# Loading half of an output projection in four-row pieces, and reordering the heads' outputs to match, in a two-layer decode kernel

## The chip, the cores and the metric

The kernel runs on one core of a Trainium2 chip. The metric is the device time of one execution in microseconds (us), from three timed runs. A core has a matrix engine (TensorE, "PE" in the profile, with its weight loads listed apart as "PEld"), a vector engine (VectorE, "DVE"), a scalar engine (ScalarE, "ACT"), a general engine (GpSimd, "POOL") and a sync engine ("SP"), whose queue issues nearly all of this kernel's loads. Each engine has its own list of instructions, and semaphores make one engine wait for another. The kernel lets PE write its products to PSUM tiles, from which DVE or ACT read them.

## The reference

Two identical decoder layers are applied to four sequences of one token each. The cache and the weights are the same in both layers. Cut to what matters:

```
B, D, Hq, Hkv, Sk, Dh, F = 4, 512, 32, 8, 4096, 128, 1792      # bfloat16

def A(x):                                   # attention over a cache
    q = (x @ wq)                            # 32 query heads of 128
    k, v = repeat(k_cache, 4), repeat(v_cache, 4)   # 8 key heads, 4 query heads each
    p = softmax(q @ k.T * Dh ** -0.5)       # 4096 positions
    o = p @ v                               # (B, Hq, 1, Dh)
    return o.reshape(B, 1, Hq * Dh) @ wo    # wo: 4096 x 512

def M(x):
    return (gelu(x @ w_gate) * (x @ w_up)) @ w_down

x = x + A(layernorm(x)); x = x + M(layernorm(x))
x = x + A(layernorm(x)); x = x + M(layernorm(x))
```

[...] The projection `wo` is 4 MB and stays on the chip once it is loaded.

## The kernel before

**Order of the work.** The kernel handles sequence after sequence. `attend_first` does layer 1 of sequence 0. `attend` is called three times; each call does layer 2 of sequence b-1 beside layer 1 of sequence b, so that the K and V tiles of a sequence are read close together. `attend_last` does layer 2 of the last sequence and ends in the output projection of layer 2 for all four sequences. `dense_first`, `dense` and `dense_last` are the feed-forward parts. The order is written out by hand (the kernel turns automatic scheduling off).

**Loads.** SP issues the loads in program order. K and V come in tiles of 512 KB, each partition reading 16 adjacent rows of 256 bytes, which is 4 KB in one piece. A V slot is handed to the next tile when its last matmul is done (`ring.pump`, L708); K tiles are issued from L518. `load_rest` (L158) loads all the weights that are needed after the first attention: first `wo` in four loads of 1 MB (L161), then the gate, up and down weights. For `wo` the row index is split as (head i, partition p), so each partition gets one row of 512 numbers, 1 KB, per query head.

**Attention values.** Class `Values` walks through V tiles (`step`). For most key heads the probabilities are the stationary operand and V is streamed past them (`stream_v`, L791); afterwards DVE transposes the result (`turn_v`, L799), sums it (L806) and scales it (L807) into the output array, in which every query head is one column of 128 partitions: `OT_bf` for layer 1, `OT2_bf` for layer 2 (four columns a head, one for each sequence). For the other heads V is the stationary operand (L859), and one DVE instruction (L680) scales. `step(n, hold=True)` puts off the DVE part until `flush()`.

**Output projection.** Six of the eight key heads go through `RowProj`: the head's column is stationary and a row block of `wo` is streamed (L405); four heads run in four 32-column strips of PE. `split` (L412 on ACT, then L413 on DVE) turns the four strips into a pair of terms, and `onto` adds them to the result of `OutProj`, which handles the last two key heads with `wo` as the stationary operand (L275). At the end `add_x` (L425) adds the projection to the residual.

**In `attend_last`** the two key heads of each pair are done in the order (2,3), (0,1), (4,5), 6, 7. The steps around the change are: `vals.step(8, hold=True)`, `soft_turn(p1)`, `vals.flush()`, the second group's swap of probabilities, two ACT fills and an ACT table load (L1291), `vals.step(4)` for heads 4 and 5, `rows.heads` for pairs (2,3) and (0,1), `vals.step(2)` for head 6, `rows.heads` for (4,5), `rows.split()`, then head 7 in two steps with head 6's projection between them, `rows.onto(proj)`, and head 7's projection.

Of the kernel before, what the change touches and what calls it, by code (L numbers as in the profile page):

```python
# [8 lines left out]
FP32 = mybir.dt.float32  # L9
# [6 lines left out]
P = 128  # L16

LN_EPS = 1e-5
QD = 4
QS = P // QD  # L20
WIDE = 32
WEIGHT = 64
# [3 lines left out]
GH = 4  # L26
# [10 lines left out]
def kernel(  # L37
# [24 lines left out]
    NT = C // CH  # L62
# [6 lines left out]
    TG = GH * NT  # L69
# [15 lines left out]
    ps_sm = ctx.enter_context(tc.tile_pool(name="ps_sm", bufs=1, space=bass.MemoryType.PSUM))  # L85
# [3 lines left out]
    dq = nc.sync  # L89

    wq_sb = [wts.tile([P, KD, HG * Dh], BF16, name=f"wq_sb{g}") for g in range(NG)]
    wo_sb = wts.tile([P, Hq, D], BF16, name="wo_sb")
# [9 lines left out]
    wo_dram = A_wo.rearrange("(i p) n -> p i n", p=P)  # L102
# [7 lines left out]
    ident_bf = const.tile([P, P], BF16, name="ident_bf")  # L110
# [38 lines left out]
    def cache_tile(cache, b, kvh, t):  # L149
        if whole(b, kvh):  # L150
            return cache[b, kvh].rearrange("(p t c) d -> t p c d", t=NT, p=P)[t]
        return cache[b, kvh].rearrange("(t p c) d -> t p c d", t=NT, p=P)[t]

    def load_wq(g):
        n = HG * Dh
        dq.dma_start(out=wq_sb[g][:], in_=wq_dram[:, :, g * n:(g + 1) * n])

    def load_rest():  # L158
        n = Hq // 4
        for i in range(4):  # L160
            dq.dma_start(out=wo_sb[:, i * n:(i + 1) * n], in_=wo_dram[:, i * n:(i + 1) * n])  # L161
        dq.dma_start(out=wg_sb[:], in_=B_w_gate.rearrange("(k p) n -> p k n", p=P))
        dq.dma_start(out=wu_sb[:], in_=B_w_up.rearrange("(k p) n -> p k n", p=P))
        wd_dram = B_w_down.rearrange("(k p e) n -> p k e n", p=P, e=2)
        wd_pairs = wd_sb.rearrange("p (k e) n -> p k e n", e=2)
        for lo, hi in zip(WD_PARTS, WD_PARTS[1:]):
            if hi - lo > 1:
                own = slice(lo // 2, hi // 2)
                dq.dma_start(out=wd_pairs[:, own], in_=wd_dram[:, own])
            else:  # L170
                dq.dma_start(out=wd_sb[:, lo], in_=wd_dram[:, lo // 2, lo % 2])
# [307 lines left out]
    def busy(count, unread, by=None, start=True, lhsT=None):  # L479
        rhs = wg_sb[:, 0] if by is None else by  # L480
        for _ in range(count):
            nc.tensor.matmul(unread, lhsT=ident_bf[:] if lhsT is None else lhsT, rhs=rhs[:, :unread.shape[1]], start=start,  # L482
                             stop=start, skip_group_check=True)
# [98 lines left out]
    def scores(sc, g, t, runs=together):  # L582
        for run in runs:
            scores_of(sc, g, [(s, t) for s in run])
# [224 lines left out]

    class Values:  # L810
        def __init__(self, layer, b, tiles, prob, dst, keeps=(), streamed=(), paired=(), sums=None, park=(),
                     last_bank=None, off_ot=False, last_width=WEIGHT):
            self.streamed, self.sums, self.park = streamed, sums or {}, park
            self.paired, self.last_bank, self.off_ot = paired, last_bank, off_ot
            self.last_width = last_width
            self.layer, self.b, self.tiles, self.n = layer, b, list(tiles), 0
            self.prob, self.dst, self.keeps = prob, dst, keeps
            self.seen, self.ot, self.late = {}, None, []
# [65 lines left out]
        def unit(self, kvh):  # L884
            pair = [2 * (kvh // 2), 2 * (kvh // 2) + 1]
            alone = kvh in self.streamed and kvh not in self.paired
            return [kvh] if self.tiles[-1][0] in pair or alone else pair

        def scale(self, ot, unit, rden):
            n, s = len(unit), unit[0] % GH  # L890
            if unit[0] in self.streamed:
                turn_v(ot, n)
                return sum_v(ot, self.dst(unit[0], n), rden[:, s:s + n], n)
            scaled(self.dst(unit[0], n), ot[:, s % 2:s % 2 + n, :rep], rden[:, s:s + n])
# [5 lines left out]
    class Streamed:  # L900
# [30 lines left out]
        def sum(self):  # L931
            kvh, ps = self.sums.pop(0)
            g, s = divmod(kvh, GH)
            sum_v(ps, self.dst(kvh, 2), self.prob[g][1][:, s:s + 2], 2)
# [22 lines left out]
    hp = 2 * rep  # L957

    def attend_first():

        b, (gx, gy) = 0, first_groups[0]
        prob1 = {}
        keys = Keys(b, (gx, gy))
        kept, own, other, _ = two(b)
        last = one(b)[-1][0]
        vals = Values(1, b, one(b), prob1, dst1(b), keeps=kept,
                      streamed=[h for h in range(Hkv) if h != last],
                      paired=[h for h in range(Hkv) if h // 2 != last // 2])
        ring.extend(1, b, one(b))
        load_wq(gx)  # L970
        keys.load_heads(GH)
        load_wq(gy)
        keys.load(TG)
        ring.pump()
        make_identity(nc, ident_bf[:])
        build_consts()
        xT_ps = ps_sm.tile([P, KD, B], BF16, name="xT_ps", tag="sm")
        for k in range(KD):
            nc.tensor.transpose(xT_ps[:, k, :], x_bf[:B, k * P:(k + 1) * P], ident_bf[:B, :B])
        nc.vector.tensor_copy(out=xb[:, :, :B], in_=xT_ps[:])  # L980
# [12 lines left out]
        q_first(gx)  # L993
        q_build(q1_bf[:, gx, :, b])
        sc1 = new_scores()
        for s in range(GH):
            keys.turn(NT)
            for t in range(NT):
                scores_of(sc1, gx, [(s, t)])
        p0 = soft(sc1)  # L1000
        q_first(gy)
        soft_turn(p0)
        q_build(q1_bf[:, gy, :, b])
        pe, den = soft_swap(p0), soft_den(p0)
        keys.turn()
        prob1[gx] = (pe, soft_recip(den))
        keys.turn(3)
        vals.step(2)
        sc1 = new_scores()
        scores(sc1, gy, 0, last_alone)  # L1010
        keys.turn(4)
        vals.step(3)
        scores(sc1, gy, 1, last_alone)
        vals.step(3, hold=True)
        p0 = soft(sc1)
        vals.flush()
        soft_turn(p0)
        prob1[gy] = (soft_swap(p0), soft_recip(soft_den(p0)))
        vals.step(TG)
        assert vals.left() == 0  # L1020
        load_rest()
        scr = Scratch()
        early = Early(b + 1, second_groups[b])
        heads, twice = pairs(one(b)), o1(b)
        summed = RowProj(lambda i: twice(i).broadcast_to([P, 2]))
        for h in heads[:-1]:
            summed.heads(h, hp)
        summed.split(scr.words.bitcast(BF16))
        proj = OutProj(o1(b), 1)
        proj.heads(heads[-1], rep)  # L1030
        summed.onto(proj)
        proj.n = Hq - rep
        proj.heads(heads[-1] + rep, rep)
        ring.extend(2, b, own)
        return proj.y, early, scr
# [99 lines left out]
    def attend(b, qy, before, norm, early=None):  # L1135
# [11 lines left out]
        vals1 = Values(1, b, one(b), prob1, dst1(b), keeps=kept1,  # L1147
                       streamed=[gy * GH + s for s in range(GH - 1)], park=apart1,
                       sums={4: (ps_sc, "sc"), 5: (ps_sm, "sm"), 6: (ps_sc, "sc")},
                       last_bank=lambda: ps_sm.tile([P, 2, WEIGHT], FP32, name="ot", tag="sm"))  # L1150

        sc2 = [new_scores(early=True)]
        if early:
# [59 lines left out]
        turn(4)  # L1213
        vals1.step(3)
        scores(sc1, gy, 1, last_alone)
        p0 = soft(sc1)
        vals1.step(3)
        x = swap_tile()
# [4 lines left out]
        heads = pairs(one(b))  # L1223
# [10 lines left out]
        vals1.step(1)  # L1234
        proj = OutProj(o1(b), 1)
        spare = proj.bank[:, KD * WEIGHT:]
        rows.heads(heads[2], rep)
        busy(3, spare)
        vals1.step(1)
        rows.heads(heads[2] + rep, rep)  # L1240
        rows.split()
        busy(5, spare)
        vals1.step(1)
        proj.heads(heads[3], rep)
        vals1.step(1)
# [6 lines left out]
    def attend_last(q_bf, norm, before, late):  # L1252
# [5 lines left out]
        vals = Values(2, b, tiles, prob2, dst2(b),  # L1258
                      streamed=[h for h in range(Hkv) if h != tiles[-1][0]],
                      paired=[h for h in range(Hkv) if h // 2 != tiles[-1][0] // 2],  # L1260
                      last_width=WIDE)
        sc2 = [new_scores(early=True)]
        scores(sc2[0], gx, 0)
        ring.pump_tile(late[0], k_tile(gx * GH + 2, 0))
# [24 lines left out]
        for part in full:  # L1289
            nothing(part[:])  # L1290
        nc.scalar.preload_act_table_set("gelu_apprx_tanh_and_others")  # L1291
        vals.step(4)
        rows.heads(heads[0], hp)
        rows.heads(heads[1], hp)
        vals.step(2)
        rows.heads(heads[2], hp)
        rows.split()
# [1 line left out]
        proj = OutProj(o2, B, WIDE)  # L1299
        proj.heads(heads[3], rep)  # L1300
        vals.step()
        rows.onto(proj)
        proj.n = Hq - rep
        proj.heads(heads[3] + rep, rep)
        part = banks.tile([P, UP_ROWS * WIDE], "ur")
        nothing(part[:])
        spare = ps_sc.tile([P, 512], FP32, name="spare", tag="sc")
# [265 lines left out]
```

## Time and profile before

| | |
|---|---|
| three timed runs | 267.55, 268.86, 269.77 us (median 268.86) |
| the profiled execution: device time | 268.99 us |
| its span, first to last instruction | 267.2 us |
| PE / DVE / ACT busy | 195.1 / 182.2 / 66.0 us |
| DMA packets, bytes | 30732, 103.05 MB, mean 386 GB/s |
| packets of the main load queue as a share of 16 engines' span | 95.7% |
| packets under 2 KB | 7144 |
| chain that ended last, by engine | DMA 51%, PE 21%, DVE 16%, SP's queue 6% |
| `wo` loads, issue to landing | 12.0 us median |
| V tiles, issue to landing | 8.5 us median |

The profile shows one execution. A window row gives, for a stretch in us from the span's start, the busy time of each engine (number of instructions in brackets), the granted PE clock, the busy share of the DMA engines and GB/s. A timeline row gives start, duration of the group, engine, source line, operation, output and inputs, shapes and count; in square brackets stands the idle time before it and what ended it. The chain that ended last is followed back from the last instruction, each step to what released it.

### The profile page before, as it was taken

The page shows a single profiled execution, that of the slowest core. Times are in us where ns is not written, and L with a number is a line of the kernel's source. Part 1 is how long each engine was busy: PE and PEld are TensorE (multiplying, and loading weights), DVE is VectorE, ACT ScalarE, POOL GpSimd, SP SyncE. Part 2 cuts the span into 40 slices and gives each one's busy share as a digit, 9 for nine tenths or more (in the row PEclk, how much of TensorE's full clock was granted, in tenths as well). Part 3 has the DMA queues.
Part 4 walks back from the last instruction along what each step waited for, and adds up shares of the span by engine and source line. Part 5 has one row for each costly group of instructions (what it writes and reads, how often), then busy time and mean ns, then how long its engine had stood idle before and what let it go on. Part 6 is the DMA issues. An engine that isn't in the chain of part 4 may idle for free.

```text
span 267.2 us, 8596 instructions
## 1 busy us (share of the span) xinstructions
PE 195.1 (73%) x3767; PEld 114.8 (43%) x3775; DVE 182.2 (68%) x448; ACT 66.0 (25%) x136; POOL 3.9 (1%) x10
## 2 busy tenths in 40 slices
PE   1396246544689796989678968787788687888884
PEld 1333123322255453557436245464363354553563
DVE  3385955451335899884776998746769996568773
ACT  1001001100222422032323520304136103044642
POOL 2000000000001000000000000000000000000001
PEclk9998555655597959799999985899999979999999
DMA  7999999999994999999999999999999999999940
GB/s 244 432 416 421 423 429 417 408 385 406 413 412 177 394 416 417 420 417 400 390 414 416 416 419 421 416 415 375 403 418 418 421 415 418 420 405 405 413 160 3
DMA packets 30732, 103.05 MB, mean 386 GB/s; under 512 B 2788, under 2 KB 7144, under 8 KB 29672
## 3 DMA queue, kind: packets, MB, share of 16 engines
q1 hardware_dynamic: 30672, 102.51, 95.7%
q8 instruction: 29, 0.48, 0.6%
q14 instruction: 7, 0.06, 0.1%
q10 hardware_dynamic: 24, 0.01, 0.0%
HBM read 102.50 MB, written 0.00 MB: 384 GB/s over the span
## 4 chain that ended last, share of the span: by engine, by line
DMA 51%; PE 21%; DVE 16%; SPq 6%; ACT 3%; issue 3%; DVEq 0%
DMA v_t<-in_A_v_cache_dram 25%; DMA kp<-in_A_k_cache_dram 8%; DMA kw<-in_A_k_cache_dram 8%; PE sc L592 6%; DMA wu_sb<-in_B_w_up_dram 5%; DMA kw<-in_A_v_cache_dram 4%; SPq L161 4%; DVE kp L537 3%; PE ot L859 3%; DVE kw L537 3%; PE y L275 3%; PE so L791 2%; PE q L309 1%; DVE q L315 1%; DVE qb L360 1%
## 5 line engine op out<-in xcount | busy, mean ns | idle before, releaser
L592 PE MATMUL sc<-kw,qb 128*32 128x512 bf16 x244 | 39.6, 446 | 5.2 <-DVE kw L537 2.2
L592 PE MATMUL sc<-kp,qb 128*32 128x512 bf16 x268 | 40.1, 450 | 1.0 <-DVE kp L537 0.2
L592 PEld LDWEIGHTS <-qb 128*32 128x32 bf16 x512 | 23.1, 104 | 39.6 <-issue 21.4
L537 DVE STREAM_TRANSPOSE kw<-kw 128x1024 f32<-128x1024 f32 x32 | 38.0, 1215 | 0.7 <-DMA kw<-in_A_k_cache_dram 0.6
L537 DVE STREAM_TRANSPOSE kp<-kp 128x1024 f32<-128x1024 f32 x32 | 36.7, 1199 | 0.0
L859 PE MATMUL ot<-pe,v_t 128*128 128x32 bf16 (+1 forms) x896 | 30.0, 184 | 5.6 <-DMA v_t<-in_A_v_cache_dram 2.8
L859 PEld LDWEIGHTS <-v_t 128*128 128x128 bf16 x896 | 27.7, 100 | 13.7 <-issue 7.4
L614 ACT ACTIVATE pe<-sc,nl 128x512 bf16<-128x512 f32 x8 | 5.5, 687 | 85.9 <-DVE pe L611 67.6
L791 PE MATMUL so<-v_t,pe 128*32 128x256 bf16 x304 | 15.0, 319 | 13.6 <-DMA v_t<-in_A_v_cache_dram 11.6
L799 DVE STREAM_TRANSPOSE so<-so 128x512 f32<-128x512 f32 (+1 forms) x23 | 13.8, 599 | 11.1 <-PE so L791 11.1
L791 PEld LDWEIGHTS <-pe 128*32 128x32 bf16 x320 | 9.1, 105 | 19.4 <-issue 12.5
L602 DVE TENSOR_REDUCE pe<-sc 128x1 f32<-128x512 f32 x12 | 8.3, 691 | 9.2 <-PE sc L592 9.1
L405 PE MATMUL yr<-wo_sb,OT_bf 128*2 128x512 bf16 (+1 forms) x120 | 10.7, 425 | 4.9 <-DMA wo_sb<-in_A_wo_dram 4.9
L647 PE MATMUL x<-pe,ident_bf 128*32 128x128 bf16 x192 | 5.4, 233 | 11.8 <-DVE pe L622 11.8
L647 PEld LDWEIGHTS <-ident_bf 128*32 128x32 bf16 x256 | 5.3, 100 | 16.1 <-issue 14.1
L791 PE MATMUL so<-v_t,pl 128*32 128x256 bf16 x192 | 9.4, 275 | 3.3 <-DMA v_t<-in_A_v_cache_dram 3.3
L650 ACT CAST pe<-x 128x512 bf16<-128x512 f32 x12 | 7.0, 586 | 17.4 <-PE x L647 17.4
L275 PE MATMUL q<-xb,wq_sb 128*128 128x5 bf16 (+1 forms) x192 | 5.7, 173 | 6.5 <-DMA wq_sb<-in_A_wq_dram 6.5
L353 PE MATMUL qe<-q_bf,ident_bf 128*32 128x16 bf16 (+1 forms) x272 | 5.7, 176 | 5.6 <-DVE q_bf L335 2.9
L622 DVE STREAM_TRANSPOSE pe<-pe 128x512 bf16<-128x512 bf16 x12 | 8.4, 696 | 1.1 <-ACT pe L614 1.1
L275 PEld LDWEIGHTS <-wo_sb 128*128 128x128 bf16 x160 | 7.6, 101 | 3.3 <-DMA wo_sb<-in_A_wo_dram 2.6
L482 PEld LDWEIGHTS <-ident_bf 128*128 128x128 bf16 x63 | 5.2, 99 | 8.7 <-issue 4.3
(172 smaller groups left out, 255.2 us busy)
## 6 DMA issues: line engine op xcount, KB each, us to landing
v_t<-in_A_v_cache_dram SPq DMA_DIRECT2D x89, 512.0 KB, 8.5
kp<-in_A_k_cache_dram SPq DMA_DIRECT2D x32, 512.0 KB, 9.9
kw<-in_A_k_cache_dram SPq DMA_DIRECT2D x24, 512.0 KB, 9.6
wq_sb<-in_A_wq_dram SPq DMA_DIRECT2D x2, 2048.0 KB, 7.7
kw<-in_A_k_cache_dram SPq DMA_DIRECT2D x4, 1024.0 KB, 11.6
v_t<-in_A_v_cache_dram SPq DMA_DIRECT2D x4, 1024.0 KB, 14.2
wo_sb<-in_A_wo_dram SPq DMA_DIRECT2D x4, 1024.0 KB, 12.0
wq_sb<-in_A_v_cache_dram SPq DMA_DIRECT2D x3, 1024.0 KB, 11.8
```

The source lines that it names most:

```text
L161: dq.dma_start(out=wo_sb[:, i * n:(i + 1) * n], in_=wo_dram[:, i * n:(i + 1) * n])
L275: nc.tensor.matmul(dst, lhsT=lhsT, rhs=rhs, start=first, stop=last, skip_group_check=True)
L405: nc.tensor.matmul(self.rows[j:j + x.shape[1]], lhsT=x, rhs=wo_sb[:, i], start=self.n < QD, stop=True, skip_group_check=True)
L537: nc.vector.transpose(out=words, in_=words)
L592: nc.tensor.matmul(sc[s * QS:(s + 1) * QS], lhsT=qb[:, w0:w0 + 2 * W], rhs=kt[:, :, be // 2, :, be % 2], start=(t == 0 and be == 0), stop= ...
L602: nc.vector.tensor_reduce(out=m, in_=sc.rearrange("p c j -> p (c j)"), axis=AX.X, op=ALU.min if norm else ALU.max)
L622: nc.vector.transpose(out=flat, in_=flat)
L647: nc.tensor.matmul(x[a * QS:(a + 1) * QS, s], lhsT=ident_bf[:, s * QS:(s + 1) * QS], rhs=pT[:, a], start=True, stop=True, skip_group_check ...
L650: nc.scalar.copy(out=pe, in_=x.rearrange("p s t c h -> p (s t c h)"))
L791: nc.tensor.matmul(ps[d, :NW * QS], lhsT=x[:, w:w + NW].rearrange("p c h -> p (c h)"), rhs=v[:, i:i + NW, d], start=first and i == 0, stop ...
L799: nc.vector.transpose(out=flat, in_=flat)
L859: nc.tensor.matmul(self.ot[:, s % 2], lhsT=v[:, i, :], rhs=wide(pe[:, s, t * CH + i, :], self.ot.shape[-1]), start=(done == 0 and i == 0), ...
```

## The change: four adjacent rows a partition for key heads 0, 1, 4 and 5

For these four key heads (16 of the 32 query heads, half of `wo`) the load gives partition p the four adjacent rows 4p to 4p+3 of the key head's 512 rows, 4 KB in one piece. The other half is loaded as before. The output columns of these heads must then hold, in partition p, the numbers 4p to 4p+3 of the key head's 512 outputs. `regroup` does this with 16 small matmuls: every fourth column of the identity picks one of four places, for each of four query heads, into one strip of 32 PSUM partitions. One ACT copy writes the result back over the same columns. Where the head's columns are written is unchanged; `regroup` is called twice in each of the five attention passes that end in a projection. Around the calls some steps are reordered.

```diff
+    def by_quads(kvh):
+        return kvh % GH < 2
...
     def load_rest():
         n = Hq // 4
-        for i in range(4):
-            dq.dma_start(out=wo_sb[:, i * n:(i + 1) * n], in_=wo_dram[:, i * n:(i + 1) * n])
+        wo_quads = A_wo.rearrange("(i p j) n -> p i j n", p=P, j=QD)
+        to_quads = wo_sb.rearrange("p (i j) n -> p i j n", j=QD)
+        for kvh in range(0, Hkv, 2):
+            if by_quads(kvh):
+                dq.dma_start(out=to_quads[:, kvh:kvh + 2], in_=wo_quads[:, kvh:kvh + 2])
+            else:
+                i = kvh * rep
+                dq.dma_start(out=wo_sb[:, i:i + n], in_=wo_dram[:, i:i + n])
...
+        def regroup(self):
+            kvh, n = self.due[0][1][0], sum(len(unit) for _, unit in self.due)
+            ps = self.due[-1][0]
+            self.due = []
+            if len(ps.shape) == 3:
+                ps = ps.rearrange("p a b -> p (a b)")
+            o = self.quads[:, kvh * rep:(kvh + n) * rep].rearrange("p (v h) b -> p v h b", h=rep)
+            nb = o.shape[3]
+            turned = ps[:, :n * QD * nb].rearrange("p (v j b) -> p v j b", j=QD, b=nb)
+            for j in range(QD):
+                for h in range(rep):
+                    nc.tensor.matmul(turned[h * QS:(h + 1) * QS, :, j], lhsT=ident_bf[:, j::QD],
+                                     rhs=o[:, :, h], start=True, stop=True, skip_group_check=True)
+            nc.scalar.copy(out=o, in_=turned)
+
         def scale(self, ot, unit, rden):
             n, s = len(unit), unit[0] % GH
+            if self.quads is not None and by_quads(unit[0]):
+                self.due.append((ot, unit))
...
@@ attend_first
         vals.step(3, hold=True)
+        vals.regroup()
         p0 = soft(sc1)
...
-        vals.step(TG)
-        assert vals.left() == 0
+        vals.step(2 * NT + 1)
+        vals.regroup()
+        vals.step(vals.left())
         load_rest()
...
@@ attend
         scores(sc1, gy, 1, last_alone)
+        vals1.regroup()
         p0 = soft(sc1)
...
         spare = proj.bank[:, KD * WEIGHT:]
-        rows.heads(heads[2], rep)
+        vals1.regroup()
+        busy(5, spare)
+        vals1.step(1)
+        rows.heads(heads[2], hp)
+        rows.split()
         busy(3, spare)
-        vals1.step(1)
-        rows.heads(heads[2] + rep, rep)
-        rows.split()
-        busy(5, spare)
         vals1.step(1)
         proj.heads(heads[3], rep)
...
@@ attend_last
         nc.scalar.preload_act_table_set("gelu_apprx_tanh_and_others")
+        vals.regroup()
         vals.step(4)
         rows.heads(heads[0], hp)
         rows.heads(heads[1], hp)
+        vals.regroup()
         vals.step(2)
         rows.heads(heads[2], hp)
         rows.split()
...
         vals.step()
+        proj.n = Hq - rep
+        proj.heads(heads[3] + rep, rep // 2)
         rows.onto(proj)
-        proj.n = Hq - rep
-        proj.heads(heads[3] + rep, rep)
+        proj.heads(heads[3] + rep + rep // 2, rep // 2)
```

`busy(n, ...)` issues n matmuls whose result is not read.

More of the change, by code (lines that the diff above doesn't have):

```diff
@@ L811, in __init__ @@
         def __init__(self, layer, b, tiles, prob, dst, keeps=(), streamed=(), paired=(), sums=None, park=(),
-                     last_bank=None, off_ot=False, last_width=WEIGHT):
+                     last_bank=None, off_ot=False, last_width=WEIGHT, quads=None):
+            self.quads, self.due = quads, []
             self.streamed, self.sums, self.park = streamed, sums or {}, park
@@ L967, in attend_first @@
                       streamed=[h for h in range(Hkv) if h != last],
-                      paired=[h for h in range(Hkv) if h // 2 != last // 2])
+                      paired=[h for h in range(Hkv) if h // 2 != last // 2],
+                      quads=OT_bf.unsqueeze(2))
         ring.extend(1, b, one(b))
@@ L1149, in attend @@
                        sums={4: (ps_sc, "sc"), 5: (ps_sm, "sm"), 6: (ps_sc, "sc")},
-                       last_bank=lambda: ps_sm.tile([P, 2, WEIGHT], FP32, name="ot", tag="sm"))
+                       last_bank=lambda: ps_sm.tile([P, 2, WEIGHT], FP32, name="ot", tag="sm"),
+                       quads=OT_bf.unsqueeze(2))
         sc2 = [new_scores(early=True)]
@@ L1260, in attend_last @@
                       paired=[h for h in range(Hkv) if h // 2 != tiles[-1][0] // 2],
-                      last_width=WIDE)
+                      last_width=WIDE, quads=OT2_bf)
         sc2 = [new_scores(early=True)]
```

## The prediction

> **What bounds the kernel now.** I read the windows first, then the chain that ended last, then the timeline of the two stretches that the chain singles out. The windows (columns: stretch, busy time of PE, PEld, DVE, ACT and POOL, granted PE clock, DMA share, GB/s):
>
> ```profile
> 48.00:50.00 2.00, 1.63 (x34) 1.08 (x34) 0.26 (x1) 1.02 (x2) 0.00 (x0) 0.75 1.03 416
> 56.00:58.00 2.00, 0.94 (x8) 0.23 (x9) 2.00 (x5) 0.00 (x0) 0.00 (x0) 0.50 1.09 386
> 58.00:60.00 2.00, 0.32 (x8) 0.10 (x7) 1.02 (x4) 0.00 (x0) 0.00 (x0) 0.50 1.09 386
> 176.00:180.00 4.00, 3.86 (x79) 3.11 (x78) 1.74 (x5) 0.59 (x1) 0.00 (x0) 1.00 1.03 418
> ```
>
> The DMA engines are full nearly all the time. V tiles move at 416 to 418 GB/s, in pieces of 4 KB; while `wo` moves in pieces of 1 KB (53 to 62 us) the share is as high, 1.09, but the rate is 386. So these pieces cost DMA time, not waiting time. Does that time reach the end? The chain says so:
>
> ```profile
> 59.84 14.06 DMA wu_sb<-in_B_w_up_dram
> 73.94 0.96 PE u L1323 x16
> ...
> 125.34 5.46 DMA v_t<-in_A_v_cache_dram
> ...
> 133.25 0.32 PE qe L353 x16
> ...
> 246.32 11.96 DMA kw<-in_A_v_cache_dram
> ```
>
> The up weights, which queue behind `wo`, land at 73.9 and the feed-forward part of sequence 0 hangs on them; later K and V loads carry the chain until the last half tile of V lands at 258.3. After that a tail of 9 us has no load in it. Whoever lengthens the tail pays in full. Its beginning, in the timeline:
>
> ```profile
> 253.83 1.06 PE L791 MATMUL so<-wq_sb,pl 128*32 128x256 bf16 x32 [0.36 <-ACT pl L650]
> ...
> 254.68 0.18 DVE L807 TENSOR_TENSOR OT_bf<-ov,rden 128x8 bf16<-128x8 f32 x1
> ...
> 254.94 0.73 DVE L799 STREAM_TRANSPOSE so<-so 128x512 f32<-128x512 f32 x1
> ...
> 255.84 0.62 PE L791 MATMUL so<-wq_sb,pl 128*32 128x256 bf16 x16
> 255.97 0.18 DVE L807 TENSOR_TENSOR OT_bf<-ov,rden 128x8 bf16<-128x8 f32 x1
> ...
> 258.73 0.17 DVE L680 TENSOR_TENSOR OT_bf<-ot,rden 128x4 bf16<-128x4 f32 x1 [0.42 <-PE ot L859]
> ...
> 259.54 0.18 DVE L425 TENSOR_TENSOR xb<-XX,y 128x16 bf16<-128x16 f32 x1 [0.63 <-PE y L275]
> ```
>
> PE streams V for heads 4 and 5 at 253.83 while DVE is still summing heads 0 and 1, whose output is complete only at 254.86 (L807). Today nothing on PE needs it before the second half of the row projections.
>
> **The load.** 2.10 MB of `wo` change from 1 KB to 4 KB pieces. At 386 GB/s they take 5.43 us, at the 418 of the V windows 5.02: a gain of 0.4 us. Bounds: nothing, if the piece were not what costs; 0.55 us at the 430 GB/s of the fastest window (34 to 36 us). I take 0.4, from the nearest row (same 4 KB by 128 partitions, same queue). The up weights then land 0.4 us earlier, the K loads of the next sequence are released 0.4 us earlier, and from there the loads run on without a pause to 258.3, so the last landing moves to 257.9.
>
> [...]
>
> **The small matmuls.** Ten regroups add 160 matmuls, 160 weight loads and 10 ACT copies. The trace has no such group, but `q_sums` (L353) has the same form: 128x32 stationary picked out of the identity, a few moving columns, four strips side by side; 16 of them fill 0.32 us of the chain at full clock. Singly such a row lasts 169 ns, so the upper bound is 2.7 us a regroup. I take 0.3, twice that at the 0.5 clock of the first 70 us. For the copy the nearest ACT rows are 0.16 us (128x4) and 0.27 us (128x128); I take 0.2.
>
> **Where they are hidden.** Sequence 0: PE waits for V tiles at 50.6, 51.8 and 53.2 and then for `wo` itself, so both regroups lie beside DMA work. In `attend`, the first regroup stands before the softmax, where PE next idles 0.78 us for DVE (before L647 at 116.94) and ACT has been idle 8.9 us; its inputs were scaled a microsecond earlier. Queued behind it are three V tiles and five dummy matmuls, which end later by 0.3 us and have that gap to use. The second regroup needs head gy1's sum, ready at 120.46, when PE gets there at 120.0: 0.45 us of waiting and 0.3 of work. The five dummies cover the ACT copy, and the displaced row matmuls are the same eight. The projection so ends about 0.6 us later. Behind it on PE are the V tiles whose release lets SP issue loads. The chain shows the price: a tile issued at 125.34 lands 5.46 us later, while a K tile issued into an idle queue (at 83.1) took 3.2. About 2.2 us of queue stand in front of it, so 0.6 us later is no idle DMA, and PE waits for V landings further on in any case. In the last call, V landings already hold PE back at 228.8 and 230.1. I count nothing for all this.
>
> **The tail.** Here nothing hides it. On the time axis of before:
> - Regroup 1 stands ahead of `vals.step(4)`. PE, in order, waits for 254.86, works 0.3, and starts heads 4 and 5 at 255.2 instead of 253.83: 1.4 us late. The ACT copy waits for the table load (254.45 to 255.73), which is early enough for the row projection.
> - Heads 4 and 5 are in PSUM at 256.3 (1.06 us for the 32), and their three DVE steps take 1.2 us (254.94 to 256.15 before): ready at 257.5. PE reaches regroup 2 at 256.95 (0.88 for the V matmuls, 0.86 for 16 row matmuls), waits, and is through at 257.85. Head 6 starts there instead of at 255.84: 2.0 us late.
> - From here PE no longer waits for landings, which gives some of it back. Head 6's output comes 1.57 us after its start (255.84 to 257.41), at 259.4; its 16 projection matmuls take 0.42; head 7's second tile ends near 260.3 and L680 starts near 260.5, against 258.73.
> - Before, `onto`'s four matmuls ran while L680 did; now they stand behind it, between two halves of head 7: 20 matmuls instead of 16, 0.1 us. `split` (ACT 0.59, DVE 0.75) ends near 260.3, just in time.
> - `add_x` (L425) starts at 261.4 against 259.54: 1.9 us late. All that follows is unchanged.
>
> **Sum.** The work that leads up to the tail comes 0.4 us earlier, the tail gets 1.9 us longer: +1.5 us. The profiled execution's 268.99 (span 267.2) becomes 270.5; it stood 0.13 above the median of 268.86, so I predict **270.3 us**, 0.55% more.
>
> **Rivals.**
> - *The tail absorbs it.* If only regroup 1's wait counts and the rest fits into the waits for landings (PE idle before 255.84, 257.04, 258.32), the tail grows by 0.8 instead of 1.9: 269.3; if nothing shows, the load's gain stays: 268.4. For: PE is idle about 1 us in all there. Against: regroup 1 alone moves PE's remaining work past the last landing. Chance 0.18 together.
> - *The load does not get faster*, because the pieces stay at 1 KB or because their size is not what cost: 270.7. The 386 of two windows with a full share speaks against it. Chance 0.08. [...]
> - *The small matmuls do not overlap*, the case that is clearly slower. Place: the two regroups of the tail, where every nanosecond counts, and then the second regroup of each `attend` call, where the loads run dry once PE is more than 2.2 us late. At half overlap (1.3 us each) the tail gains 2 us more: 272.3. At the upper bound of 2.7 us the tail gains 4.8 and each of three calls 0.95 (2.7 and 0.45 of waiting, less 2.2): 278. It decides from 0.9 us a regroup on, where the sum passes 1%. Against it stand the 0.32 us for 16. Chance 0.10.
>
> The forecast itself has 0.64. Two runs of this kernel cannot be told apart within about 1% (the three runs lie 0.8% apart). Below 266.2 lies no case, since the load can give 0.55 us at most: 0.03. Above 271.5 lie the last rival and a part of the forecast's upper side: 0.13. The rest, 0.84, is within 1%. The range reaches from 268.4 (gain kept, tail hidden) to 271.9 (each tail regroup at 0.6 us, the half-clock cost, and the spread of the runs); only the last rival is outside.
>
> **What would show it.** Main-queue packets fall by 1536, and the stretch from 53 to 62 has parts at 416. The up weights land near 73.5 and the last V half near 257.9. In the tail PE idles 0.7 to 1.1 us before regroup 1 and about 0.6 before regroup 2, released by DVE L807's counterpart, and `add_x` starts about 261.0. In `attend` the DMA share stays near 1 after each projection. I am wrong if regroup 1 finds its input ready, if 16 small matmuls take clearly more than 0.3 us, or if the up weights land no earlier.

## The result: 0.58% slower, and the tail hangs on another chain

| | before | after |
|---|---|---|
| device time, median of 14 runs (us) | 269.01 (267.55 to 271.08) | 270.52 (269.57 to 275.02) |
| ratio, 95% interval | | 1.0058 (1.0037 to 1.0080) |
| profiled execution: device time / span (us) | 268.99 / 267.2 | 270.36 / 268.6 |
| packets of the main load queue | 30672 | 29136 |
| packets under 2 KB | 7144 | 5096 |
| first matmul on the up weights (us) | 73.94 | 73.56 |
| last half tile of V landed (us) | 258.28 | 258.42 |
| last `add_x` starts (us) | 259.54 | 260.90 |

One run of 275.02 us lies far from the other 13 and is left out of the ratio. Forecast were 270.3 us and a last `add_x` at about 261.0.

The time is gained early and lost late. The early part stands in the windows of the changed kernel (columns as in the prediction: stretch, busy time of PE, PEld, DVE, ACT, POOL, granted PE clock, DMA share, GB/s):

```profile
54.00:56.00 2.00, 1.36 (x23) 1.04 (x20) 0.42 (x2) 0.00 (x0) 0.00 (x0) 0.50 1.03 398
56.00:58.00 2.00, 1.00 (x8) 0.23 (x9) 2.00 (x4) 0.00 (x0) 0.00 (x0) 0.50 1.10 399
58.00:60.00 2.00, 0.41 (x10) 0.10 (x8) 1.12 (x4) 0.00 (x0) 0.00 (x0) 0.50 1.03 415
60.00:62.00 2.00, 0.64 (x8) 0.12 (x1) 0.00 (x0) 0.00 (x0) 0.00 (x0) 0.50 1.05 387
```

The four `wo` loads alternate between 4 KB and 1 KB pieces, and the rate alternates with them: 415 where a 4 KB load is alone, 387 where a 1 KB load is. Before it was 386 throughout (53 to 62 us).

The late part is best seen in the chain that ended last. The page's line of it by engine, for the changed kernel:

```profile
DMA 36%; DVE 25%; PE 22%; SPq 9%; ACT 4%; issue 3%; DVEq 0%
```

Before, DMA had 51% of that chain and DVE 16%, and its last DMA step was the load of the last V tile, 246.32 to 258.28. In the changed kernel the same stretch of the chain holds no DMA at all (columns: start, duration, what):

```profile
250.77 0.88 ACT pl L623 x2
...
251.67 0.71 DVE pl L631
252.38 0.62 DVE so L808
...
253.47 0.64 DVE so L808
...
254.62 0.30 PE so L910 x12
254.93 0.95 PE so L800 x32
255.89 0.74 DVE so L808
...
257.15 0.30 PE so L910 x16
257.45 0.48 PE so L800 x16
```

From the softmax on it is a relay of DVE and PE: DVE turns and sums heads 2, 3 and then 0, 1 (L808 to L816), PE regroups (L910) and only then streams V for heads 4 and 5 (L800), DVE turns and sums those, PE regroups again. The last V landing has dropped out. The lines that answer to those shown of the tail before, from the timeline of the changed kernel (start, duration, engine, line, operation, idle before and its releaser in brackets):

```profile
254.39 0.18 DVE L816 TENSOR_TENSOR OT_bf<-ov,rden 128x8 bf16<-128x8 f32 x1
...
254.62 0.30 PE L910 MATMUL so<-OT_bf,ident_bf 128*32 128x8 bf16 x16 [1.45 <-DVE OT_bf L816]
...
254.79 1.06 PE L800 MATMUL so<-wq_sb,pl 128*32 128x256 bf16 x32
...
256.92 0.18 DVE L816 TENSOR_TENSOR OT_bf<-ov,rden 128x8 bf16<-128x8 f32 x1
257.15 0.30 PE L910 MATMUL so<-OT_bf,ident_bf 128*32 128x8 bf16 x16 [0.44 <-DVE OT_bf L816]
...
257.28 0.63 PE L800 MATMUL so<-wq_sb,pl 128*32 128x256 bf16 x16
...
260.90 0.18 DVE L434 TENSOR_TENSOR xb<-XX,y 128x16 bf16<-128x16 f32 x1 [0.76 <-PE y L284]
```

PE idles 1.45 us for the DVE scaling before regroup 1 and 0.44 us before regroup 2. Each regroup itself fills 0.30 us. Head 6 (L800 x16) starts at 257.28 where it started at 255.84.

### The profile page after: what moved, and what is told of

Read it like the earlier page. It is cut to its first block, busy times and chain, and to the rows that moved or that the text cites. A ratio compares the mean times of both kernels' runs of the same rounds, so it can differ in the third digit from the quotient of the medians.

```text
span 268.6 us, 8937 instructions
## 1 busy us (share of the span) xinstructions
PE 196.3 (73%) x3927; PEld 118.2 (44%) x3935; DVE 182.5 (68%) x448; ACT 67.6 (25%) x146; POOL 3.9 (1%) x10
## 2 busy tenths in 40 slices
DMA packets 29199, 103.09 MB, mean 384 GB/s; under 512 B 2788, under 2 KB 5096, under 8 KB 28136
## 3 DMA queue, kind: packets, MB, share of 16 engines
q1 hardware_dynamic: 29136, 102.51, 95.1%
## 4 chain that ended last, share of the span: by engine, by line
DMA 36%; DVE 25%; PE 22%; SPq 9%; ACT 4%; issue 3%; DVEq 0%
DMA v_t<-in_A_v_cache_dram 17%; DMA kp<-in_A_k_cache_dram 16%; DVE kp L546 5%; PE sc L601 5%; DVE kw L546 4%; DMA wd_sb<-in_B_w_down_dram 4%; PE so L800 4%; PE ot L869 3%; SPq L178 3%; PE y L284 3%; SPq L167 2%; DVE so L808 2%; SPq L171 1%; PE q L318 1%; PE yr L414 1%
## 5 line engine op out<-in xcount | busy, mean ns | idle before, releaser
L601 PE MATMUL sc<-kp,qb 128*32 128x512 bf16 x268 | 39.4, 441 | 1.8 <-DVE kp L546 0.9
L601 PEld LDWEIGHTS <-qb 128*32 128x32 bf16 x512 | 22.2, 103 | 39.3 <-issue 21.4
L800 PE MATMUL so<-v_t,pe 128*32 128x256 bf16 x304 | 15.4, 330 | 12.3 <-DMA v_t<-in_A_v_cache_dram 10.2
L808 DVE STREAM_TRANSPOSE so<-so 128x512 f32<-128x512 f32 (+1 forms) x23 | 13.8, 599 | 14.1 <-PE so L800 14.0
L800 PEld LDWEIGHTS <-pe 128*32 128x32 bf16 x320 | 9.4, 110 | 18.1 <-issue 13.4
L656 PE MATMUL x<-pe,ident_bf 128*32 128x128 bf16 x192 | 5.6, 240 | 10.8 <-DVE pe L631 10.7
L656 PEld LDWEIGHTS <-ident_bf 128*32 128x32 bf16 x256 | 5.2, 102 | 15.6 <-issue 11.2
L800 PE MATMUL so<-v_t,pl 128*32 128x256 bf16 x192 | 9.0, 274 | 1.9 <-DMA v_t<-in_A_v_cache_dram 1.9
L912 ACT CAST OT_bf<-so 128x8 bf16<-128x8 f32 (+1 forms) x7 | 1.2, 171 | 31.6 <-PE so L910 31.6
```

What stands on the lines that cost most here:

```text
L601: nc.tensor.matmul(sc[s * QS:(s + 1) * QS], lhsT=qb[:, w0:w0 + 2 * W], rhs=kt[:, :, be // 2, :, be % 2], start=(t == 0 and be == 0), stop= ...
L656: nc.tensor.matmul(x[a * QS:(a + 1) * QS, s], lhsT=ident_bf[:, s * QS:(s + 1) * QS], rhs=pT[:, a], start=True, stop=True, skip_group_check ...
L800: nc.tensor.matmul(ps[d, :NW * QS], lhsT=x[:, w:w + NW].rearrange("p c h -> p (c h)"), rhs=v[:, i:i + NW, d], start=first and i == 0, stop ...
L808: nc.vector.transpose(out=flat, in_=flat)
```

## The experiments

The theory: the load gains about 0.4 us, the two regroups of the last pass cost 1.5 to 1.9, and those of the other passes are hidden. The rivals: the load gains nothing, or the middle passes pay too, or the loss is not in the waits but in the small matmuls or in the clock. Each kernel was timed in five rounds, beside the kernel before and on the same chip. There were three batches, each on another chip, so a difference between two batches is less sure than one inside a batch; the median of the kernel before is 268.79 us for e1 to e4, 268.55 for e5 and e7 to e9, and 268.66 for e11 to e14 (269.01 beside the runs of the result above). The ratios are the record's own and not quotients of the medians: for e1 the medians give 0.9971.

| label | what differs | median (us) | ratio to before, 95% |
|---|---|---|---|
| e1_load_only | before, with the new load alone | 268.00 | 0.9949 (0.9922 to 0.9976) |
| e2_load_all | before, with all of `wo` in 4 KB pieces | 267.58 | 0.9944 (0.9918 to 0.9969) |
| e4_old_load | after, with the old load | 271.04 | 1.0070 (1.0044 to 1.0095) |
| e3_no_tail | after, no regroup in the last pass | 268.98 | 1.0000 (0.9967 to 1.0033) |
| e7_tail_only | before, with the change of the last pass alone | 270.42 | 1.0070 (1.0047 to 1.0093) |
| e8_no_middle | after, no regroup in the middle passes | 270.55 | 1.0065 (1.0039 to 1.0091) |
| e13_no_middle_no_tail | after, regroups in the first pass alone | 269.23 | 1.0017 (0.9990 to 1.0044) |
| e5_sum_first | after, heads 0, 1 summed before 2, 3 | 270.56 | 1.0080 (1.0051 to 1.0109) |
| e9_all_moved | e5 with other regroups moved later | 274.63 | 1.0207 (1.0167 to 1.0246) |
| e11_sum_first_own_bank | e5, and heads 4, 5 in a PSUM bank of their own | 269.34 | 1.0034 (1.0011 to 1.0058) |
| e12_moved_again | e11 with two regroups moved later | 269.53 | 1.0042 (1.0017 to 1.0068) |
| e14_filled_wait | after, with PE busy during the first wait | 270.38 | 1.0067 (1.0042 to 1.0091) |

### The load: alone, doubled, undone

Alone (e1, on the kernel before; the columns of the heads stay in the old order, so the projection is not the reference's):

```diff
-        for i in range(4):
-            dq.dma_start(out=wo_sb[:, i * n:(i + 1) * n], in_=wo_dram[:, i * n:(i + 1) * n])
+        for kvh in range(0, Hkv, 2):
+            if by_quads(kvh):
+                dq.dma_start(out=to_quads[:, kvh:kvh + 2], in_=wo_quads[:, kvh:kvh + 2])
+            else:
+                i = kvh * rep
+                dq.dma_start(out=wo_sb[:, i:i + n], in_=wo_dram[:, i:i + n])
```

> The kernel before with the new load alone: no regrouping, old order of steps (the four key heads meet the wrong rows of wo, so the output is another one; the work is that of before). Theory of the prediction: 0.4 us less than before, which stands at 269.0, so 268.6; the up weights land near 73.5 instead of 73.9 and the last half tile of V near 257.9 instead of 258.3. Rival, pieces of 1 KB cost nothing: 269.0 and 73.9. Rival, the gain is made at the load and lost again between 126 and 136 us, where the loads wait for slots: 73.5, but 269.0.

Doubled (e2): all four loads take the first branch.

> Twice the dose: all four loads of wo in pieces of 4 KB, otherwise the kernel before (all heads but their order meet the wrong rows, so the output is another one). Theory of the prediction: twice the gain, 0.8 us, 268.2, up weights at 73.1. If the gain is lost on the way: no less than the run with half of it.

Undone (e4, on the changed kernel): the lines of e1's diff the other way round.

> The changed kernel with the old load, regroups and order as changed (four key heads meet the wrong rows, so the output is another one). Theory of the prediction: 0.4 us more than the changed kernel, 270.9. If the load's gain does not reach the end: 270.5.

At the load itself all the profiles agree, and the dose shows. From the moment when 21 MB had landed to that when 32 MB had, a stretch that holds all of `wo`, the trace's DMA records give:

| `wo` in 4 KB pieces | profiles | 21 to 32 MB (us) |
|---|---|---|
| none | before, e4, e7 | 27.33 to 27.35 |
| half | after, e1, e3, e5, e8, e9, e11, e12, e13, e14 | 26.85 to 26.94 |
| all | e2 | 26.47 |

That is 0.44 us for 2.1 MB and 0.88 for 4.2. The windows of e2 over the stretch shown above:

```profile
54.00:56.00 2.00, 1.25 (x20) 0.93 (x17) 0.52 (x2) 0.00 (x0) 0.00 (x0) 0.50 1.03 424
56.00:58.00 2.00, 1.02 (x8) 0.23 (x9) 2.00 (x5) 0.00 (x0) 0.00 (x0) 0.50 1.02 418
58.00:60.00 2.00, 0.68 (x8) 0.23 (x8) 1.02 (x4) 0.00 (x0) 0.00 (x0) 0.50 1.02 420
60.00:62.00 2.00, 0.57 (x8) 0.10 (x7) 0.00 (x0) 0.00 (x0) 0.00 (x0) 0.50 1.03 422
```

With no 1 KB piece left the whole stretch moves at 418 to 424 GB/s. The rival "the load does not get faster" falls. What the gain is worth at the end is less sharp. Alone it gives 0.8 us by the medians (0.6 to 2.1 by the interval of the ratio), more than the load itself gains; where the rest comes from is not shown. Undoing it in the changed kernel costs 0.5 by the medians, with intervals that overlap. The double dose is 0.4 us faster than the single one by the medians, with intervals that overlap nearly whole.

### The last pass: without it, and alone

Without (e3; heads 0, 1, 4 and 5 of the last projection stay in the old order, so their part of the output is another one):

```diff
         nc.scalar.preload_act_table_set("gelu_apprx_tanh_and_others")
-        vals.regroup()
         vals.step(4)
         rows.heads(heads[0], hp)
         rows.heads(heads[1], hp)
-        vals.regroup()
         vals.step(2)
```

> The changed kernel without the two regroups of the last pass, all else as changed (the last pass leaves the order of four key heads as it is, so the output is another one). Theory of the prediction: the tail pays 1.65 to 1.9 us for these two, so 268.7 to 268.9 against 270.5 for the changed kernel, and add_x starts near 259.3. Rival, the tail would absorb them and the time is lost in the middle: 270.5.

Alone (e7, on the kernel before): the two calls, the scaling's list for them, and the new order of head 7's projection, with the old load everywhere.

> The kernel before with only the last pass changed: its two regroups and its new order of steps, old load (four key heads of the last pass meet the wrong rows, so the output is another one). The kernel before stands at 268.8. Theory of the prediction: 1.65 to 1.9 us more, 270.4 to 270.7. Rival, the tail costs less when the lead of the loads is not there: under 270.

Without its two regroups the changed kernel takes 268.98 us, 1.5 less than with them. Alone, the last pass makes the kernel before 1.9 us slower (270.42 against 268.55). What the tail hangs on can be read from two differences in each profile: from the last V landing to the last `add_x`, and from the `add_x` ahead of it (the end of the feed-forward part before the last pass) to the last one.

| profiles | after the last V landing (us) | after the `add_x` ahead (us) |
|---|---|---|
| before, e1, e2: no regroup in the last pass | **1.26, 1.26, 1.27** | 18.76, 18.27, 18.22 |
| e3, e13: no regroup there, new order of head 7 | **1.38, 1.38** | 19.62, 18.79 |
| after, e5, e8, e9, e14: regroups | 2.48, 1.82, 2.33, 2.25, 3.46 | **20.41, 20.33, 20.41, 20.26, 20.43** |
| e4, e7: regroups, half clock in the tail | 4.09, 3.73 | **21.44, 21.29** |
| e11, e12 (below): regroups, own bank for heads 4 and 5 | 1.39, 2.21 | 19.36, 19.58 |

In each of the first four rows one of the two hardly moves. Without the regroups the end follows the last landing; with them it follows the compute chain by 20.3 to 20.4 us, whenever V lands (by 21.3 to 21.4 at half clock). The chain of waits of e3 has the same look as that of before:

```profile
245.92 12.67 DMA kw<-in_A_v_cache_dram
...
258.63 0.38 PE ot L869 x8
...
259.03 0.17 DVE OT_bf L689
```

One DMA step of 12.67 us stands where the changed kernel has its relay of DVE and PE.

### The middle passes: without, and without the last as well

In e8 the six calls `vals1.regroup()` are taken out of `attend` (their heads then enter layer 1's projections in the old order); in e13 those of the last pass as well.

```diff
         scores(sc1, gy, 1, last_alone)
-        vals1.regroup()
         p0 = soft(sc1)
...
-        vals1.regroup()
         busy(5, spare)
```

> The changed kernel without the two regroups of each of the three middle passes; order of steps, new load and the other four regroups as changed (in layer 1 of three sequences four key heads meet the wrong rows, so the output is another one). Theory of the prediction: they are hidden, 270.5. Rival, from the runs of the load alone (268.0) and of the change without the tail's regroups (269.0): the middle passes give back about 1 us of what the load gains, so 269.5 to 269.7; the loads then lose less between 126 and 136 us than in the changed kernel.

> The changed kernel without the regroups of the last pass and of the three middle passes; new load, new order of steps and the two regroups of the first pass stay (the output is another one). The run without the last pass's regroups alone took 269.0, the load alone 268.0. If the middle regroups are what lies between: 268.0. If it is the order of steps, or nothing but scatter: 268.7 to 269.0.

Taking the six out gains nothing: 270.55 against 270.52 with the last pass's regroups in place, 269.23 against 268.98 without them. This although the chain of the changed kernel goes through one of them (119.54, 0.30 us, L910), and although the row shows a wait:

```profile
119.54 0.30 PE L910 MATMUL so<-OT_bf,ident_bf 128*32 128x2 bf16 x16 [0.34 <-DVE OT_bf L816]
```

The projection of sequence 1, from the swap of probabilities (L647 before, L656 after) to `add_x`, takes 8.57 us in the profile of the change and 8.06 in that of before. But this difference cannot be put down to the regroups: without them the same stretch takes 8.54 us in e1 and 9.15 in e13. Over all profiles but that of e9, the medians with the six regroups and without them are 8.56 and 8.30 us in the first of the three middle passes, 9.10 and 9.17 in the second, and 9.13 and 9.21 in the third.

### The wait in the last pass: handed on, then removed

If regroup 1's wait is the cost, heads 0 and 1 can be summed ahead of heads 2 and 3 (e5):

```diff
         soft_turn(p1)
+        vals.late.reverse()
         vals.flush()
```

> The changed kernel with one edit in the last pass: DVE sums heads 0 and 1 before heads 2 and 3, so that the first regroup's input is there when PE comes to it. Theory of the prediction, that the wait for DVE is what the first regroup costs: PE starts heads 4 and 5 about 1.0 us earlier against the swap of probabilities before it, and the time falls by 0.9 to 1.1 us, to 269.4 to 269.6. Rival, the 16 matmuls and the second regroup are the cost: 270.3 to 270.5.

No gain: 270.56. The timeline of e5 shows that the wait was only handed on:

```profile
254.24 0.30 PE L910 MATMUL so<-OT_bf,ident_bf 128*32 128x8 bf16 x16 [0.60 <-DVE OT_bf L816]
...
254.85 0.22 DVE L815 TENSOR_REDUCE ov<-so 128x8 f32<-128x64 f32 x1
...
255.17 1.06 PE L800 MATMUL so<-wq_sb,pl 128*32 128x256 bf16 x32 [0.64 <-ACT gr L383]
```

Regroup 1 waits 0.60 instead of 1.45 us, but now heads 4 and 5 wait 0.64. The row names an ACT fill (L383), which had ended at 254.6. What ended just ahead of the start is DVE's sum of heads 2 and 3 (254.85 to 255.07). The kernel uses two PSUM banks in turn for these results, so heads 4 and 5 are written to the bank that heads 2 and 3 are read from. To test that reading, e11 gives heads 4 and 5 a bank of their own:

```diff
-                      last_width=WIDE, quads=OT2_bf)
+                      last_width=WIDE, quads=OT2_bf, sums={4: (ps_sc, "sc")})
...
         soft_turn(p1)
+        vals.late.reverse()
         vals.flush()
```

> The changed kernel with heads 0 and 1 summed first, as in the run before, and with heads 4 and 5 in a PSUM bank of their own, so that they need not wait until heads 2 and 3 are summed out of the shared bank. Theory, that the wait was handed from the regroup to the bank: PE starts heads 4 and 5 0.65 us earlier than there, measured from the swap of probabilities, and no gap of over a microsecond is left on PE in the tail; the time falls by 0.6 to 0.9 us to 269.6 to 269.9. Rival, the tail is bound elsewhere: 270.5.

269.34 us, 1.2 less than e5 and than the change. In the timeline of e11 heads 4 and 5 no longer wait; they start 1.22 us after the swap of probabilities, in e5 2.26:

```profile
252.90 0.30 PE L910 MATMUL so<-OT_bf,ident_bf 128*32 128x8 bf16 x16 [0.35 <-DVE OT_bf L816]
...
253.04 1.06 PE L800 MATMUL so<-wq_sb,pl 128*32 128x256 bf16 x32
...
253.54 1.28 ACT L1324 ACT_TABLE_LOAD   x1
...
254.00 1.67 PE L414 MATMUL yr<-wo_sb,OT_bf 128*4 128x512 bf16 x16
...
254.83 0.18 ACT L912 CAST OT_bf<-so 128x32 bf16<-128x32 f32 x1
...
255.50 0.27 PE L910 MATMUL so<-OT_bf,ident_bf 128*32 128x8 bf16 x16
```

Its last `add_x` comes 19.36 us after the `add_x` ahead, where e5 has 20.33, and 1.39 after the last V landing. The chain that ended last still runs through DVE and PE in this profile, but the landing, at 257.83, now falls among the last V matmuls (257.63 to 258.24): the two end nearly together. So the waits for DVE carry most of the tail's cost, not the small matmuls, which are all still there. What is late next can be seen as well: the ACT copy (L912) stands behind the table load, and the 16 row matmuls, half of which need it, take 1.67 us instead of 1.05. A table load behind the copy was not tried.

In e14 PE does six unread matmuls during regroup 1's wait, without changing the wait:

```diff
         nc.scalar.preload_act_table_set("gelu_apprx_tanh_and_others")
+        fill = ps_sc.tile([P, 512], FP32, name="fill", tag="sc")
+        busy(6, fill[:])
         vals.regroup()
```

> The changed kernel with six dummy matmuls ahead of the last pass's first regroup: PE waits for DVE as long as before (the idle 1.45 us are filled with 1.3 us of work that nobody reads). In two of the profiles with these regroups the granted PE clock was 0.5 for 3.4 us from 255 us on and the tail 1.0 us longer. If the idle gap brings that about in a part of the executions: no half clock between 250 and 262 us, the lowest times as in the changed kernel (269.6), the median 0.2 to 0.5 us lower, 270.0 to 270.3. If the gap has nothing to do with it: 270.5.

270.38, not to be told from 270.52. In the change the granted clock is 1.00 in all windows from 250 to 262; in e14 the 32 V matmuls of heads 4 and 5 and the 16 row matmuls behind them take 1.06 and 1.05 us, as in the change, and the tails are equally long (20.43 and 20.41 us): the wait costs this much without any fall of the clock.

### Regroups moved later

e9 is e5 with the regroups put behind more work, so that their inputs are ready when PE gets there: in `attend` the first one behind three V tiles and the second behind the dummy matmuls, in the last pass the second one behind head 6.

```diff
-        vals1.regroup()
         p0 = soft(sc1)
         vals1.step(3)
+        vals1.regroup()
         x = swap_tile()
...
-        vals1.regroup()
         busy(5, spare)
+        vals1.regroup()
...
         soft_turn(p1)
+        vals.late.reverse()
         vals.flush()
...
-        vals.regroup()
         vals.step(2)
+        vals.regroup()
+        vals.step()
         rows.heads(heads[2], hp)
         rows.split()
-        vals.step()
```

> The whole change with every regroup put where its input is ready: the sum of heads 0 and 1 first and the second regroup behind head 6's stream in the last pass; in the middle passes the first regroup behind the three V tiles, the second behind the five dummy matmuls. Same output as the changed kernel. If waits are what the regroups cost: the load's 0.8 us stay, the tail pays about 0.6 (20 instead of 16 last matmuls, split later) and the middle 0.2 to 0.4, so 268.5 to 269.0, level with the kernel before (268.8). If the matmuls themselves cost: 270 or more.

4.1 us slower than the change. The timeline of e9 in the first of the three middle passes:

```profile
115.42 0.14 ACT L912 CAST OT_bf<-ot 128x8 bf16<-128x8 f32 x1
...
115.60 0.69 DVE L563 TENSOR_SCALAR park<-v_t 128x512 int32<-128x512 int32 x1 [1.22 <-ACT OT_bf L912]
116.20 0.70 DVE L631 STREAM_TRANSPOSE pe<-pe 128x512 bf16<-128x512 bf16 x1
...
116.95 0.41 PE L656 MATMUL x<-pe,ident_bf 128*32 128x128 bf16 x16 [1.43 <-DVE pe L631]
```

In the change the ACT copy runs at 113.05, in a stretch in which ACT has nothing else. Moved, it queues behind the exponential of the softmax and runs at 115.42. DVE's parking copy (L563) waits 1.22 us, by the profile for it, the transpose of the probabilities (L631) stands behind that, and PE idles 1.43 us. After that the granted clock falls from 1.00 to 0.60 and 0.54, as the windows of e9 show:

```profile
116.00:118.00 2.00, 0.73 (x18) 0.53 (x18) 2.00 (x5) 0.64 (x2) 0.00 (x0) 1.00 1.04 420
118.00:120.00 2.00, 1.95 (x36) 1.26 (x40) 1.63 (x6) 0.00 (x1) 0.00 (x0) 0.60 1.02 408
120.00:122.00 2.00, 2.00 (x31) 0.91 (x24) 0.82 (x3) 0.00 (x0) 0.00 (x0) 0.54 0.98 363
```

`add_x` of sequence 1 starts at 126.85 instead of 124.53, and by the DMA records 53 MB have landed at 138.13 instead of 135.66: here the loads follow the compute chain. Up to the next swap of probabilities the delay grows to 5.3 us (146.28 against 140.94), and from there on it stays between 4.3 and 5.4. So in this profile the loss arises in the first middle pass; the second has the same wait of 1.43 us and loses nothing more.

e12 is e11 with the second regroup of `attend` behind the dummies, as in e9, and the last pass's second regroup behind head 6.

```diff
-        vals1.regroup()
         busy(5, spare)
+        vals1.regroup()
...
-        vals.regroup()
         vals.step(2)
+        vals.regroup()
         rows.heads(heads[2], hp)
```

> The same, and the second regroup of the last pass behind head 6's stream, and the second regroup of the middle passes behind the five dummy matmuls (the first of the middle passes stays where the change has it, ahead of the softmax). If waits are the cost: 0.3 us off the tail and 0.3 off a middle pass where it shows, 269.0 to 269.4, near the kernel before (268.6 to 268.8). If moving the middle one was what cost four microseconds in the run with everything moved: over 272.

269.53, not to be told from e11's 269.34. Since the second regroup of `attend` can stand behind the dummies at no cost, what is left to explain the 4 us of e9 is the first, with its copy on ACT. This is argued from the profile of e9; the first regroup moved alone was not run.

No version that computes the whole reference beat the kernel before. The best of them, e11, is 0.34% slower than it (0.11 to 0.58%).

## Why the prediction was right, point by point

The sum was right: 270.3 forecast, 270.52 measured, inside 268.4 to 271.9, and slower by 0.58% with a forecast of 0.55. Its terms did not all hold, and the closeness owes something to luck. Ahead of the tail 0.4 us was to be gained, but e3, which lacks only the last pass's regroups, stands level with the kernel before; the tail was to cost 1.9 us and costs 1.5 against e3. The two differences, both within the noise, cancel. Single times of a profile that came out as forecast prove little for the same reason.

- **The load, −0.4.** Right where it arises: 0.44 us in ten profiles against three. The up weights' first matmul, forecast at 73.5, starts at 73.56; it lies between 73.29 and 73.90 in the ten and between 73.90 and 74.04 in the three. The rate for 4 KB pieces was forecast as 418 and is 418 to 424 in e2, 8 to 10% above the 386 GB/s of the 1 KB pieces before. Its worth at the end was under-sized if e1 is asked: 0.8 us by the medians, at least 0.6 by the interval.
- **The small matmuls, 0.3 us for 16.** Right: 0.30 in every tail at full clock, 0.27 in e11. The ACT copy was forecast as 0.2 and takes 0.14 to 0.19. The slower rival ("the small matmuls do not overlap") falls with that.
- **Hidden in the middle, 0.** Right in its sum (e8, and e13 against e3). That the projection ends 0.6 us late is not shown: the medians above put it 0.3 us later in the first of the three passes, within a scatter of over 1 us, and not later in the other two. **The reason for hiding it did not hold**: the step that said that 2.2 us of queue stand in front of the transfers. In e9 a projection that is 2.3 us late puts the landings 2.5 us late, at 138.13 us for 53 MB, where the other thirteen profiles have 134.7 to 136.3; 2.2 us in reserve would have left almost nothing of that. The DMA share, which was to stay near 1, is 0.90 and 0.92 in the windows of the change from 128 to 132 us (305 and 313 GB/s, before 387 and 395). But these regroups need not be the cause: e4, which has them too, has a share of 0.99 and 1.00 there (342 and 326 GB/s). Why a delay of some tenths costs nothing stays open.
- **The tail, +1.9.** Right in its mechanism and its size: 1.5 (change against e3) and 1.9 (e7 against before) by the medians, 1.65 in the two profiles (20.41 against 18.76). The last figure depends on when V lands: the profiles whose tail hangs on the landing have 18.2 to 19.6 us. PE's waits were forecast as 0.7 to 1.1 and 0.6 us and are 1.45 and 0.44; the first contains 0.36 that PE waited there before. The last `add_x` was put at 261.0 and starts at 260.90.
- **The last V landing at 257.9.** Not confirmed: 258.42 in the profile of the change, and, e9 apart, from 256.36 (e1) to 259.46 (e5) in the profiles with the new load, so that one of them cannot show a shift of 0.4. This is the step that let the load's gain run on without a pause up to the end. Whether it does made no difference here, since the tail no longer follows that landing.
- **Rival "the tail absorbs it".** It falls: by the table of differences the end no longer follows the last landing, as the argument against this rival said.

One thing stays open. By the medians the new load alone makes 268.00, while the change without the regroups of the middle and of the last pass makes 269.23; only the first pass's regroups, the new order of steps around the calls and head 7's order (0.1) lie between the two. The two kernels were timed on different chips, but their ratios to before are apart too (0.9949 and 1.0017). With the old load the same kind of comparison shows nothing by the ratios: the change of the last pass alone has 1.0070, everything but the load has 1.0070 (by the medians 270.42 and 271.04, again on two chips). So either the new order costs about 1 us that the old load hides, or the gain of the load does not add up with the rest; the runs do not tell which.

## What to carry to other kernels

When an engine's work is put ahead of its other work and needs the last result of another engine, count the wait and then follow the whole relay, because two waits of 1.45 and 0.44 us took the end off the last load and hung it on a compute chain. Before moving such a step later, see what its copy then stands ahead of in another engine's queue (e9), and before bringing its input forward, see what shares a buffer with what is put back (e5 and e11). Two differences, one from the last landing and one from the last result ahead of the tail, tell in one look which of the two a tail hangs on.

## What the runs showed of the hardware that was not expected

**A wait of 1.4 us was followed by half the clock in e4, e7 and e9, and by the full clock in the change.** The timeline of e4, whose tail has the same instructions as that of the change:

```profile
255.55 0.30 PE L904 MATMUL so<-OT_bf,ident_bf 128*32 128x8 bf16 x16 [1.45 <-DVE OT_bf L810]
...
255.72 1.90 PE L794 MATMUL so<-wq_sb,pl 128*32 128x256 bf16 x32
...
257.38 1.93 PE L408 MATMUL yr<-wo_sb,OT_bf 128*4 128x512 bf16 x16
```

The 32 V matmuls take 1.90 us (1.06 in the change) and the 16 row matmuls 1.93 (1.05). The windows of e4 carry the clock:

```profile
256.00:258.00 2.00, 2.00 (x40) 1.43 (x36) 0.34 (x1) 0.55 (x2) 0.00 (x0) 0.50 0.70 266
258.00:260.00 2.00, 2.00 (x56) 1.02 (x44) 0.82 (x4) 0.18 (x1) 0.00 (x0) 0.71 0.02 8
```

The granted clock is 0.5 for 3.4 us from 255.7 on, and the tail is 1.0 us longer for it (21.44 against 20.41). The profile of e7 has the same for 3.4 us from 255.1 on (0.77, 0.50 and 0.87 in the windows from 254 to 260), behind a wait of 1.44 us, and that of e9 for 3.4 us from 118.4 on (0.60 and 0.54 in the windows shown above), behind 1.43. The change has the wait of 1.45 us too, and its clock is 1.00 in all windows from 250 to 262; e8 has the same wait, and its 32 V matmuls and 16 row matmuls take 1.06 and 1.05 us, as in the change. What decides between the two is not shown: no run was made to find it. The prediction named a "half-clock cost" in its range, without saying what brings it about. How much of this cost lies in the medians is not shown: e14, which keeps PE busy there, is not faster.

**The releaser that the profile names was the wrong one in e5.** It puts the wait of heads 4 and 5 (0.64 us) down to an ACT fill that had been done for over half a microsecond (254.6, with the start at 255.17). The bank that they share with DVE's input was the cause: with a bank of their own, in e11, the wait is gone, and the kernel is 1.2 us faster (269.34 against 270.56).
